# Three edits at once in a convolution-and-gated-unit backward kernel: a new layout of the inverse spectra in DRAM, more of the hidden activations stored, another order of the first loads

## The chip, the cores and the metric

The kernel runs on one core of a Trainium2 chip. The core has TensorE (matrix products into PSUM, called PE in the profile), VectorE (DVE), ScalarE (ACT), GpSimd (POOL), and SyncE (SP), whose queue here issues every data transfer; 16 DMA engines move the data between DRAM and the on-chip memory SBUF. The metric is the time of one execution on the device in microseconds. The time before the change is the median of three runs, 442.43 us (441.31 to 444.41).

## The reference

For 2,048 tokens of width 512 the reference computes the sum of the input, a convolution block and a gated block, both on the normalized input, and then the gradients of that sum with respect to all inputs but one:

```
xn  = layernorm(q)
k_s = causal convolution of k over 4 tokens with shift_k     # per channel
kv  = k_s * v
y   = irfft(rfft(kv, 4096) * rfft(ssm_k, 4096))[:2048]       # long convolution
A   = xn * (y + kv * ssm_D)
h   = (xn @ w_gate) * (xn @ w_up)                            # width F = 1376
out = q + A + h @ w_down
grads = vjp(out)(grad_out)   # q, k, v, shift_k, ssm_k, ssm_D, w_gate, w_up, w_down
```

All data are bfloat16. The long convolution is computed with Fourier transforms written as matrix products, for three signals at once: the filter (with ssm_D added to its first tap), kv, and the incoming gradient dy = xn * grad_out. Three products of the spectra, transformed back, give y, the gradient of kv and the gradient of the filter.

## The kernel before

The 2,048 tokens lie in 16 rows of 128 partitions (R = 16). The work has these stages.

- **First loads and layernorm.** The program queues loads of x, of grad_out transposed (goT), of grad_out (go) and of the weights of the first step (L341 to L355). Warm-up products of a tile of ones run on TensorE meanwhile (L317 to L323). `ln` (L369) makes mean and variance of a row on VectorE, a square root on ScalarE, a reciprocal, and normalizes the row. `tr_rows` (L384) transposes two rows on TensorE.
- **The gated block in steps of F.** F is cut into six steps (NST, of 256 columns and one of 96). Step j runs over the 16 rows two at a time (`mlp_rows`, L391): grad_out times w_down, and xn times w_gate and w_up, then products on VectorE into a ring of SBUF buffers of 24 rows. From the ring come the weight gradients (`dw_gen`, L534). For the last stage the three results per row (h and two gradients) are needed transposed. Steps 0 to 3, and of step 4 the rows below KEEP = 8, are written to a DRAM tensor HD (`hd_store`, L408). The rest stays in the ring: rows 8 to 15 of step 4 and all of step 5, which `turn_gen` (L559) transposes on TensorE, eight blocks of 128x128 at a time, each eight copied back by ScalarE.
- **Stages A and S, the transforms.** `a_gen` (L417) does the first half of the forward transform and writes to the DRAM tensor AX. `s_gen` (L518) reads it in another order, does the second half (`s_B`), multiplies spectra on VectorE (`s_pw`), does the first half of the inverse transform (`s_Bi`) and writes to the DRAM tensor CX, in 16 stores of 768 KB. CX has 128 frequency rows with 32 token rows of 3 KB each, and 64 bytes of padding after each of the 32. Between these products stand those of the gated block's steps and the weight gradients, so that TensorE has other work while one of them waits.
- **Stage F.** Eight groups n of two token rows. `c_load(n)` (L613) reads from CX, for each of 128 frequency rows, the two rows of the group from both halves of the tokens: four runs of 3 KB per partition. `last_dft` does the second half of the inverse transform. `hd_load(m)` (L579) loads row m of HD with a transposing DMA into one of two buffers for even m or the only one for odd m; it moves 640 rows (even m) or 512 (odd m) of 768 elements, and 128 fewer from m = KEEP on. `y_o` and `y_x` (L719, L732) multiply the transposed blocks with the weights wy, which `wy_load` brings in six loads. `c_load(0)` writes over buffers that the last `s_Bi` reads and needs all stores of CX to have landed.

The order in which the instructions stand is not the order of this code. A recording layer (class Eng, L142) collects operations, and `emit` (L180) puts them out in the order of the list PLAN (L32), which also fixes the PSUM banks. All engines, and SyncE's queue of transfers, work through their own share of this list in order. The profile names line 172, the recording layer, for nearly every instruction; they are told apart by tile and shape.

Of the kernel before, what the change touches and what calls it, by code (L numbers as in the profile page):

```python
# [10 lines left out]
BF = mybir.dt.bfloat16  # L11
# [6 lines left out]
S = 2048  # L18
D = 512
F = 1376  # L20
R = 16
NFB = 11
NST = 6
SW = [256, 96, 256, 256, 256, 256]
SF = [0, 1280, 256, 512, 768, 1024]
SB = [0, None, 1, 2, 3, 4]
WO = [12 * sum(SW[:j]) for j in range(NST)]
NCH = 8
RING = 24
KEEP = 8  # L30
EPS = 1e-5
PLAN = "c-lpG0~98^?{<;~UE8*8+qP}nwr$(CZQHi(y?1y2@4NSRzHg?JO!M?fnw*|aCpI7e!~uf1kOtyGd`JKe5(0yOLLxBm5CTF%C<qN<AS{G~@DKqaLL`U`Q6MTrgXoYIVn9rY1*IV|WP|Kb268|W$O-wO9^`_gkOy)@eaH(1pfV(bd{7X|LKP?kRUtW)hr&<}ia<3e3dNv06o=-J0xCcWr~x&h7Sx7H&<RpPNoWDRpboTz&d>mQLtUr{sh}0~fkx088bTZB3*Dd{^n=DQ4oX26Xae0~0i=eu&=vYaQy2>EVIcH?W-tsoz`rm6IzmsF0pnpIM8cUc9MZ!em;fVT5sZL|Fc=oYBp3yoVF;v!$uJty!5CNtOCU4Mf+?^Xrovd51505xEQ94R4d%iYSOL>vD`bIruoAYxeAo+XAOmcNeXtI8z*^V^J7GV3hV}3fzQArc02$#RY=k|q0gl2~I0VPx8)SlGa2QU)5jX+g;WC_pi|`xH!Fjj>Kj0EvfYT5U<6{C$h-aV+cEv<^4IaQ%_z8(|6LiCe&>eeVXzYoP;2*dSk0A-3qojBPlHnit1<CO&5T?MCm<m%PVj4_~PvADB!(P}ML*P^BgLj}WJ_o>I_zXtiC+LU6u|JN)QP>zAHo?)@6dA|j7z~BYP;nDB#}?QUL*hefg@&!M4TizC*bdvHU<V9~v#}#~!Z{cYJx<5YI1|I;0GxpXaTX53!8i|ZLIfOwm9R3-#amDiBVuGMgoUvP-i4yL8dqQxya&bbK19XhSOQC8DU61tu?&{Qa#$XtV+E{&Rk0dY#8ns*W8fOBj&X1$*1(#00&8JyT#K==4mO~57#m-}D_D<p@g>y5xY&^D;|6Siuc0B<p+>k7H{%-^iU+YS)uVm*7T&`+d<XSu5`KUQI36csdYp(EFe6UIop=B<;S}73hwuw!#>F@dvtU*{j7u;Z?!oMs1CL-%%!Ru#H|D{km>2WmLfnh_@fdEwMOXj_(tO;8CvhoW!K-);uj388iMMbB-Nrk(AMfHlypIp?AwI&#_ynKgR(yuf@ddub<M;|+;~RX7@9;f-z}oZ?KjCNmf?x3)e#am96aT^O_%Hs#-}nau3xJ3mF$pOdc?v-xDHMgKFcg-;QFw|#3os%@qVu>6n@~Txh!-$2?Z8Xej0R8?DoLfNDV3%&G>FPlIch=8=`s$c<dlL^QYvamsVNPmr6H7#(o+V?NSP=zWudH;jmpzdsz4Q~5@n|xv>bC%E;@z7C^zMys5FoAQa;L01*jkuqLEaXiqLc_O2w!+Ri-LbmHJaPDnY}kI@O?P6rEyFO^QjeC^p5RMsynEQap-J3Fr(?p@fu(5>paNN@uY#b);l8o?6j4>_n}pElr|{)P~yA1nNoCr~|d58PuI7Q!naFqi81epf0qEu2C&oN3&=(eWl*ChQ`ut8bj-;E3KueG@9nn2AWUZXd~^Xy)=&I(gE5{eP|z@r=_%q4$>CtOBZMbEvId?j5g6B+D<F!B5kFgw3#l^zw{67qy==D&d@K~K}YEdEvB=yhz`>++C>ZLJ3XSSbexXR54uAy=>#pI-*l2<x>zo@yHAfPj*IK!xqB4f-K7NX8zpp!Tw?cxlDMQUnfpT_+*1nUPSFDj>DYyJ&jJfT+;eL0PE&H{+zU$KLb;Sq-E|7>I=Jxe26c3uTxWNay0}}^)eUsv+<UrBgIqWFkv>p&*TeO6y<BhiiTb#{uAdv~`n%8ciiWwtE|q&juPL=l<I=ixF1>q88C*t}$z^s!To(6^vbt<;xXbQxxSXz@tM78T2CkuN<Z`>lu8C{vnz`n#g=^_RTDjKl54Uk`U0GMowR7bixI8YeLzmCxcOzT@H_4fc;wC%q3c5%xs*B(vyD2W3i|AOUy6A4S6H$rb#=0@iWSkr6LWq}XZoC`iP^P;I&Iw6espu-Xcv9I_aaG+6SIt#-A*F_^>1w&!u8y1FX1Tg9tW0$CTxgl;R=7|y-z{+~-E6nag_osnj$7`+Nf?PQtK3|-*hP>+E};~5MO;KF>LN)omq3cU$dX7(xFk~2t#(^oR7orgTvFNQO1WfGLQ1>na@{R-#bu2v<D$q7mt1bTMedfn?bf<G?ykG%V#s~>z(tdXE~ccG0WOw2a%ttUd*WitQx`{`xik`*GfNmwC(m72&LZJBgM{Z}?zlVQ(o1%Uz$qk$oOD?wm7H>?T{b!6a>`kkQqH+da^B^VGLl;^xQtR(^2kMZ$>o*H?usiXS6z9@ClUFYi^LmTMS0;0N&#8tDo7#8FaNkA@~_+IN=ji_?|!*b(ou@ZZ}-O)l}-Y@$sv~(;?1sx)RV}(#nqB19F?Q7<GNB)n1w5eas#O%`(1r$B9&#YYb?eGTr;UE`<&;dQe8rDNNy+xT_Xv_&83cPch#hYymW_LH>oW<+$+~oUc2t{#<h~Su8q8N?_CdRE1l)A`{24td->=-xg+kg`{KIDSJzs;xpvZ1zPk?6TV~4-my72}FUiKaxxWmTpDsENkQf}3vvVwt!*O|_jFxyjLUM3y9wa$=jO=tnBoD{u!IFUcNM26JyWA*A#EE&N^phmK+a={>JXVr(UrE8kWUlOSDS5oilcO#ZkCUM?QRYiJ&cK;@f=rc3vRE>5Dqbq7ISZHIX);C9a4}BLOC&ANkWyTdC(A5ZAk(EZFO*}FmGkjYDZ_<$k<66*T!0JnMp-EZxj3(qqFjzwOA)TbTcrY*<;q;1*GNU)B-MDG)ZnVTR<=nkuEI6BIxmyj{EZv%7Fi*6xj!$L0lY&t$Ur_Wb+{q#l0m#)Hp^f>AwzhNwBnO8l()+;9?m1UH6M^uvQJv@PB|loWVeju(=v+B%4j|!E&08S;k`1J&&vlH$NQxox8Z{_o-fNesn6~Bu(an6d__9)9qGiKxeH&Fu6#jmOE<nG-MI%pke=L&@5@E$&G)1a_vO2CO&&=<KEgNTp&aE2e2kCt6FI@x<s?6rTk=Jo$tnIOr}?Iw;j{cy&hb}i#4qHdyp+cLouA8j{v>bY0$=1y{7NqKXKBXo<h6X4E8LW?adZADF*TOHm5JPzf5>mS&XX8)GMi4}2mD7+RUh(Hp2kk6b11#XA+-sU{v-E!2LF-}I+Jg)*D(5TU|X8Sp*6PN=Gh!hS?6$AjiYlpg3jalyny5C4GypIbRqxXoBW6)X?%^WcX%^L(=Ggy6X;e>s8KYAZsW&%UnA;v-oc4=Cr8y?yqov%6HcUiIlAuSB)Xq7Xfi#(2l)^$;-tEm(`zbS!iRY&XVPVSM^o!^&ZsLmo37+loJO~6R$a}>HHYrdyP93s@Ke60Yk3`~)DN6RGixqQq3b!FZs3i)S3mMyPOC3?6X(-?nnz#pRnDm|d8fYSPh3EEX<mKDx%CZy=KNY%|K<1mjEm|Q{>tUFh?du1Tuh&H1udw>b+^9didsnvX$h^YRkWj4)oQv&OKK-At(~=tcGYfLO1o<h?Ww)AtoGJE+E>eHKkcu-d4TTMfjUSB>jAB<HMFMI(%M=_>*^34s`Yf3F43jBOo!_TU9Ky1rLNMax?0!hT3x5>b%Soy-?~XR>uo)#TXeEc(L*{_r|ES4hiB+aou#vNj?UG2I$sy)LS3XIb(AjF(K<%Q>Np**^>u<y)CSs6C+Sgrpj-8rHqwXsSsUwNZKAKWsXozW+FV=cBW<Zi^qIEO*7`=<=yPqWAN0C@)mPe1Z|Gyas_*ose$w`u&(7*cy{2z9k#*27dQQ)4V!Ng9^`c(T@0!G3DBC4XYA;pnhi+3fZ(+>rr-rbw7Slr6WesWJ?27)Q-}IM;xBQmOPU`?WuK#KQJEIXSmc=o$6B^NCTR|&kajm!&vUpa);@e66qa`hYozjFB$-tsoa*J%vQdnq<Vks?}MYmLz+G1E5%WByzt);UJR^D=0ddp}Ptd!-nik90lS!t_ebu61@w)$4t8dw!8Y)!1HHMKHU!&+K3%VI^WmDRPfR@7SCK+9wGtf95Bwl>JBTO%86Bdn%1wjox_Mp}0}XrrvQHM7yy&YD|$>tLO1qD`{N*3mj!PwQe+tgDT&7B<xu*gP9=)2x>*wdvNw#@aILYs+nx&9GIr$X44zTVq3Qt*x+iHq(aLdYf&F?U2o}4c5=*+78=jhi#K>wo7)zF54D6YFq7!?X;`5&92#XyJ5HOt-Z6G*3I5qF1uxSY`A@}?Y7cB+I+ifdF_+kvvT&?mKYlQFZRv8+IRb5y=|90wEOnccH206VK42KowWY;+RoZ3``7l_X}e%i{5d;gQT-E(=AYUli|!v=41dgG`s4P@`dBRg#>DTpxc<4t_UZftQ~%5M*l&yD&BycUeR%JE2LHz*`HVh-Pw3BECLiCEPwDqs0{_60`OyA^IiJ}l^%pIbKVVsWVxQV4@mYNspWTP>VSP4V#3%RRd{rOP=ke8i4iCP%&*>xjGCr3t>dX2xzML=SYxv^6yszm?_*x!)K406X^(lNEpVzna^?U_i*Vp&0d?R1kxAql%e&5cw@r8VQU%+?pp?p*Sk9G7-d^6w4m-L-|bKl1g_6>X&U&?p&-Th=g#ZUD^{50RqH}pgObl<}d^D}%;Khu}?z5E<s*w69>{cxYi_w%#;Hb34+_H%t-zua&4{rx1r!w>R1{Q$qn@A3=$2*2A`@*DjgzsZmEZT)7y*AMi${b;|!AMyMA7C*+X^ke-2zsisE^ZaVR-=FfQ{Tbib&-VxY8b8XP^)37oztEraYkhBj$e;IB{0)EDU-0Yvb-&eL_V@h*f6+hmH~k~O*kAHX{bPT{Kk>KxRlm$X_3QmL|H9w)8~ihW$3OQI{7Zk=zw#6PTmQ~~@E`qAf6O2E_xx-B-oNpm{0aZrpY&!dYHEQau<(EH0j<n|eZg4&vjt9A!V*9r@K*>7q=EL|KntGA0&sw65CAEN2A-h903757N2vYB`zzUkKtKco{Xcu41sH*t9Do8W)nG^qb^=#WG6$i+2lPJ^2Rv)gzXd6Or3B%>LxQe?mjwNBAo_nd2c-t)AIJbSXbC2x6x95`F+l&xzZMQsh&h;eaFYDj!v7;{kQsCpEY{yD1!D)R7f3LWHUG`)Zz2I#!CC!J1(OZvfC?5TVC4Vb3sz4553vrLHv"  # L32
KB = 1024


@with_exitstack
def kernel(
    ctx: ExitStack,
    tc: tile.TileContext,
    x_d: bass.AP,  # L40
    go_d: bass.AP,
    goT_d: bass.AP,
    k_d: bass.AP,
    v_d: bass.AP,
# [950 lines left out]
```

## Time and profile before

| | |
|---|---|
| median of three runs | 442.43 us (441.31 to 444.41) |
| the profiled execution, its own time | 444.42 us |
| span of the profiled execution | 442.6 us |
| TensorE busy | 423.1 us, 3,179 products |
| VectorE busy | 353.2 us |
| ScalarE busy | 266.0 us |
| DMA moved | 124.12 MB, 280 GB/s on average |
| loads of CX, 8 of 1,536 KB | 8.3 us median from issue to landing |
| stores to CX, 16 of 768 KB | 5.3 us median |
| transposed loads of HD, 16 | 8.7 us median |

Times count from the start of the span. A window's DMA share is the busy time of the 16 DMA engines over the window; as packets can overlap in an engine it can pass 1. Busy time of TensorE is taken from pipelined products whose ends are modelled. The granted clock of TensorE (PEclk) is 1.0 at full speed.

### The profile page before, as it was taken

To read this page: it belongs to the slowest core of one execution; us is meant where nothing else is said; L and a number is where in the kernel's file an instruction comes from. 1 tells how busy PE (TensorE), PEld (TensorE's weight loads), DVE (VectorE), ACT (ScalarE), POOL (GpSimd) and SP (SyncE) were. 2 spreads that over 40 slices of the span, in tenths; PEclk is the share of its full clock that TensorE was granted. 3 is DMA by queue.
4 is the path that set the end of the run, shared out by engine and by line. 5 is a ranking of instruction groups with operands and counts; after the bars stand their busy time and mean duration, and the time that the engine had idled before them with its cause. 6 is when DMAs were issued, how large, how long until landed. Compare 5 with 4: busy or idle time off the path is not lost.

```text
span 442.6 us, 8134 instructions
## 1 busy us (share of the span) xinstructions
PE 423.1 (96%) x3179; PEld 203.9 (46%) x3179; DVE 353.2 (80%) x690; ACT 266.0 (60%) x366; POOL 3.4 (1%) x9
## 2 busy tenths in 40 slices
PE   5999999999999999999999999999999888999895
PEld 3565546745445543334434345465444333444343
DVE  3889577799934899979999994055797959999897
ACT  3796778488652579999999998386324013321311
POOL 1000000000000000000000000100000000000000
PEclk9699999999999999999999999999999999999999
DMA  8988769999856768957578779999999999999992
GB/s 263 408 290 306 287 237 336 342 361 376 314 213 239 279 198 307 315 187 280 211 271 307 285 279 274 282 327 293 294 256 274 277 284 277 275 284 285 239 314 92
DMA packets 96366, 124.12 MB, mean 280 GB/s; under 512 B 53316, under 2 KB 62153, under 8 KB 96328
## 3 DMA queue, kind: packets, MB, share of 16 engines
q1 hardware_dynamic: 96328, 123.60, 87.7%
q8 instruction: 25, 0.41, 0.4%
q14 instruction: 13, 0.11, 0.1%
HBM read 56.57 MB, written 54.04 MB: 250 GB/s over the span
## 4 chain that ended last, share of the span: by engine, by line
PE 71%; DMA 16%; DVE 7%; ACT 2%; SPq 2%; issue 1%; DVEq 0%; ACTq 0%
PE PP L172 71%; DMA big<-HD 8%; DVE big L172 7%; DMA out_dram<-big 2%; DMA AX<-big 2%; ACT big L172 2%; SPq L172 2%; DMA big<-in_x_dram 2%; DMA big<-CX 2%; DVEq L991 0%; ACTq L172 0%; DVEq L172 0%
## 5 line engine op out<-in xcount | busy, mean ns | idle before, releaser
L172 PE MATMUL PP<-big 128*128 128x512 bf16 (+8 forms) x3179 | 423.1, 347 | 14.6 <-DMA big<-HD 5.3
L172 PEld LDWEIGHTS <-big 128*128 128x128 bf16 (+4 forms) x3179 | 203.9, 98 | 233.3 <-issue 69.7
L172 DVE TENSOR_TENSOR big<-big 128x1024 bf16<-128x1024 bf16 (+5 forms) x465 | 267.7, 631 | 52.8 <-ACT big L172 43.3
L172 ACT CAST big<-PP 128x1024 bf16<-128x1024 f32 (+2 forms) x311 | 224.6, 788 | 92.9 <-PE PP L172 81.4
L172 ACT ACTIVATE big<-big 128x512 bf16<-128x512 f32 (+2 forms) x28 | 18.7, 670 | 72.0 <-DVE big L172 54.5
L172 DVE CAST big<-PP 128x512 bf16<-128x512 f32 (+1 forms) x37 | 32.3, 874 | 13.0 <-PE PP L172 11.4
L172 ACT COPY big<-PP 128x1024 bf16<-128x1024 bf16 x25 | 25.1, 1038 | 6.3 <-PE PP L172 6.3
L172 DVE SCALAR_TENSOR_TENSOR big<-big 128x1 f32<-128x1 f32 (+2 forms) x52 | 25.0, 500 | 0.5
L172 DVE TENSOR_TENSOR big<-big,PP 128x512 bf16<-128x512 bf16 (+1 forms) x17 | 10.9, 652 | 7.1 <-PE PP L172 7.0
L172 DVE BATCH_NORM_STATS2 big<-big 128x6 f32<-128x512 bf16 x16 | 10.7, 678 | 6.9 <-DMA big<-in_x_dram 6.9
L172 DVE SCALAR_TENSOR_TENSOR big<-big,PP 128x512 f32<-128x512 bf16 x16 | 10.9, 684 | 4.1 <-PE PP L172 4.1
L172 DVE TENSOR_SCALAR big<-big 128x1 f32<-128x1 f32 (+1 forms) x28 | 7.0, 261 | 0.2
L172 POOL MEMSET big<- 128x1536 bf16 (+2 forms) x3 | 2.8, 950 | 279.1 <-DMA CX<-big 279.1
L172 ACT ACT_TABLE_LOAD x2 | 2.6, 1283 | 0.8 <-PEq L983 0.7
L172 DVE BATCH_NORM_AGGREGATE big<-big 128x2 f32<-128x6 f32 x16 | 2.6, 174 | 0.1
L172 DVE RECIPROCAL big<-big 128x2 f32<-128x2 f32 x8 | 1.3, 157 | 1.3 <-ACT big L172 1.3
L172 DVE DVE_READ_ACCUMULATOR big<-big,PP 128x1 f32 x16 | 1.3, 83 | 0.0
L172 DVE DVE_READ_ACCUMULATOR big<-big 128x1 f32 x16 | 1.3, 83 | 0.0
L172 DVE MEMSET big<- 128x1 f32 (+1 forms) x2 | 0.2, 112 | 0.8 <-PEq L983 0.8
L172 DVE COPY big<-PP 128x1024 bf16<-128x1024 bf16 x1 | 0.7, 692 | 0.0
masks.py:199 POOL TENSOR_SCALAR_AFFINE_SELECT big<-big 128x128 bf16<-128x128 bf16 x1 | 0.3, 294 | 0.0
masks.py:197 POOL MEMSET big<- 128x128 bf16 x1 | 0.2, 205 | 0.3 <-POOLq L983 0.3
(4 smaller groups left out, 0.4 us busy)
## 6 DMA issues: line engine op xcount, KB each, us to landing
AX<-big SPq DMA_DIRECT2D x16, 768.0 KB, 4.8
big<-AX SPq DMA_DIRECT2D x16, 768.0 KB, 5.0
CX<-big SPq DMA_DIRECT2D x16, 768.0 KB, 5.3
big<-CX SPq DMA_DIRECT2D x8, 1536.0 KB, 8.3
out_dram<-big SPq DMA_DIRECT2D x44, 256.0 KB, 3.3
HD<-big SPq DMA_DIRECT2D x14, 768.0 KB, 5.9
big<-in_v_dram SPq DMA_DIRECT2D x16, 256.0 KB, 4.7
big<-in_w_dram SPq DMA_DIRECT2D x4, 768.0 KB, 8.0
```

What stands on the lines that cost most here:

```text
L172: o.fns.append(lambda: f(*[fix(x) for x in a], **{kk: fix(x) for kk, x in k.items()}))
```

## The change

The change has these parts, and a new PLAN that orders everything anew.

- KEEP goes from 8 to 16: all rows of step 4 are written to HD. `turn_gen` has only step 5 left, two more stores of 768 KB to HD are made, and `hd_load` moves 640 or 512 rows for every m.
- CX is laid out by token chunk: 16 blocks, each of which holds 32 x 8 runs of 3 KB and 4 KB of padding. A store of `s_Bi` is split in two, of 384 KB each, one for each of the two frequency groups. `c_load(n)` reads two whole blocks, one run of 12 KB into each of the 128 partitions. The order of frequencies on partitions differs, and the tables of the two transforms are permuted to match.
- The first loads: x rows 0 and 1 come one by one, loads of x and goT alternate in smaller pieces, the load of shift_k (SK) comes last. Rows 0 and 1 have a layernorm each. The square root writes where the reciprocal is made (the tile std is gone). A square root of a constant is computed at the program's start. Sixteen of the 24 short warm-up products are taken out. The small product into c1 is issued in the loop over rows.

In SyncE's queue as it is built, the 640-row load of HD row 0 stood ahead of the last two stores of CX, and the load of row 1 ahead of the first load of CX. After the change the order is: the last stores of CX, row 0 of HD, the first load of CX, the last load of wy, row 1 of HD. Of the six loads of wy, five stand behind the second last group of stores of CX, where two did. The load of HD row 15 had 12 transfers of 256 KB or so behind it, and has 6. In VectorE's order the copy of the first transposed rows stood behind four of the layernorm sums, the last of them of a row of the third load of x; it now stands behind three, the last of them of row 2.

```diff
-KEEP = 8
+KEEP = 16
...
-    CX = dram.tile([128, 32, 3 * D + 32], BF, name="CX")[:, :, 0:3 * D]
+    CX = dram.tile([16, 256 * 3 * D + 2048], BF, name="CX")[:, 0:256 * 3 * D]
...
+    nc.scalar.activation(s1[:, 0:1], eps_t[:], ACTF.Sqrt)
...
-    for i in range(24):
+    for i in range(8):
         now[0] = -40.0 + i
         MM(at0[:, 0:128], lhsT=ones1[:], rhs=ones1[:], start=True, stop=True)
...
-    xload(0, 2); step()
+    xload(0, 1); step()
+    xload(1, 1); step()
+    gtload(1, 1); step()
     ld(Wl[0][:, 1024:3072], w_d[:, 1024:3072]); step()
     xload(2, 2); step()
-    gtload(1, 1); step()
-    xload(4, 4); step()
-    gtload(2, 2); step()
+    gtload(2, 1); step()
+    xload(4, 2); step()
+    gtload(3, 1); step()
+    xload(6, 2); step()
+    gtload(4, 2); step()
+    xload(8, 4); step()
+    gtload(6, 2); step()
+    xload(12, 4); step()
     ld(SK[:].rearrange("p j d -> p (j d)"), bass.AP(tensor=sk_d.tensor, offset=sk_d.offset, ap=[[0, 128], [1, 4 * D]])); step()
-    xload(8, 4); step()
-    gtload(4, 2); step()
-    xload(12, 4); step()
-    gtload(6, 2); step()
...
-        nc.scalar.activation(std[:, gs], mv[:, gs, 1], ACTF.Sqrt, bias=eps_t[:, 0:1], scale=1.0)
-        nc.vector.reciprocal(rstd[:, gs], std[:, gs])
-        if 2 <= r0 <= 8:
-            STT(c1[:, r0 + 1:r0 + 2], mv[:, r0 + 1:r0 + 2, 0], -1.0, rstd[:, r0 + 1:r0 + 2], op0=ALU.mult, op1=ALU.mult)
+        nc.scalar.activation(rstd[:, gs], mv[:, gs, 1], ACTF.Sqrt, bias=eps_t[:, 0:1], scale=1.0)
+        nc.vector.reciprocal(rstd[:, gs], rstd[:, gs])
         for r in range(r0, r0 + n):
             if 2 <= r0 <= 8 and r > r0:
+                STT(c1[:, r:r + 1], mv[:, r:r + 1, 0], -1.0, rstd[:, r:r + 1], op0=ALU.mult, op1=ALU.mult)
...
-            dst = CX.rearrange("(g k) r e -> (k r) g e", k=4)[:, 4 * i + 2 * s:4 * i + 2 * s + 2, :]
-            st(dst, sp["C"][s][:].rearrange("p g t d -> p g (t d)"))
+            for g in range(2):
+                dst = CX.rearrange("a (g b e) -> a g b e", g=32, b=8)[:, 4 * i + 2 * s + g]
+                st(dst, sp["C"][s][:, g].rearrange("p t d -> p (t d)"))
...
-        r0 = 2 * n
-        ld(f["C"].rearrange("q (h r) e -> q h r e", h=2), CX.rearrange("q (h r) e -> q h r e", h=2)[:, :, r0:r0 + 2, :])
+        ld(f["C"].rearrange("p r e -> p (r e)"), CX.rearrange("(j n) (x e) -> x j n e", j=2, x=64)[:, :, n])
...
-                        ln(0, 2)
+                        ln(0, 1)
+                        ln(1, 1)
```

## The prediction

> **What bounds the kernel now.** I read the page first, then the table of busy times by stage, then the list of waits in the last stage, and last the queue's and VectorE's order of time. The page shows TensorE nearly full:
>
> ```profile
> span 442.6 us, 8134 instructions
> ...
> PE 423.1 (96%) x3179; PEld 203.9 (46%) x3179; DVE 353.2 (80%) x690; ACT 266.0 (60%) x366; POOL 3.4 (1%) x9
> ...
> DMA  8988769999856768957578779999999999999992
> ```
>
> Of 442.6 us TensorE is idle in 19.5. The row of the DMA engines says where a second limit comes in: from the 25th slice on it stands at 9 without a break. The table by stage (span, PE, PEld, DVE, ACT, POOL busy, clock, DMA share, GB/s) makes that exact:
>
> ```profile
> 200.00:230.00 30.00, 30.00 (x306) 13.34 (x305) 29.37 (x54) 27.67 (x36) 0.00 (x0) 1.00 0.74 271
> 260.00:290.00 30.00, 29.82 (x235) 14.98 (x237) 10.72 (x21) 18.73 (x26) 1.41 (x2) 1.00 1.00 290
> 290.00:350.00 60.00, 59.48 (x379) 27.95 (x378) 46.36 (x90) 26.58 (x30) 0.00 (x0) 1.00 1.02 286
> 350.00:430.00 80.00, 73.14 (x371) 31.43 (x371) 71.64 (x152) 19.08 (x22) 0.00 (x0) 1.00 1.07 275
> 430.00:443.00 13.00, 7.75 (x52) 4.13 (x50) 9.98 (x25) 2.10 (x3) 0.00 (x0) 0.92 0.34 127
> ```
>
> Three stages have three answers. From about 30 to 290 us TensorE alone sets the pace (30.00 of 30.00 in the first row, DMA at 0.74). From 290 to 430, the last stage F, TensorE and the DMA engines are both at their limit: TensorE loses 0.5 us in the first 60 us and 6.9 in the next 80, 7.4 together. The last row is the end: TensorE runs out of work, and the DMA engines with it. The list of waits in that stage names what it waits for (engine, releaser: us in total, times, longest):
>
> ```profile
> PE PP L172 <- DMA big<-HD: 5.3, 6, 1.5
> PE PP L172 <- DMA big<-CX: 1.3, 2, 1.1
> PE PP L172 <- ACT big L172: 1.0, 2, 0.8
> ```
>
> So the transposed loads of HD, which the change lengthens, are the very thing TensorE waits for. The third place is the start, on VectorE:
>
> ```profile
> 9.13 0.70 DVE L172 BATCH_NORM_STATS2 big<-big 128x6 f32<-128x512 bf16 x1 [1.83 <-DMA big<-in_x_dram]
> ...
> 11.29 0.69 DVE L172 BATCH_NORM_STATS2 big<-big 128x6 f32<-128x512 bf16 x1 [0.54 <-DMA big<-in_x_dram]
> 11.95 0.69 DVE L172 COPY big<-PP 128x1024 bf16<-128x1024 bf16 x1
> ```
>
> The copy of the first transposed rows stands in VectorE's order behind a layernorm sum that waits for x rows 4 to 7; TensorE's first gate/up product starts at 12.70.
>
> **The change part by part.** Sums are made against the profiled execution: 444.42 us, of which 442.6 are the span and 1.8 lie around it. The median of the runs shown is 442.43; I carry the difference over to it.
>
> *All of step 4 stored.* Removed are 48 transposes (8 rows, 3 tensors, 2 blocks) and 6 ScalarE copies of 1,038 ns. A group of 8 transposes shows 0.6 us busy with 219 ns for a single one, so they follow each other at (0.6 - 0.219) / 7 = 54 ns: 48 x 54 = 2.6 us of TensorE, in a stretch where it was busy 29.82 of 30. All of it is on the path: **-2.6**. The copies (6.2 us) go from an engine that is busy 18.73 of 30 there: 0. Added are two stores of 768 KB into HD in the stage with DMA at 0.74: they lie beside TensorE's work, 0. They would cost their 5.9 us each to land only if a load behind them in the queue were late there, and TensorE waits for no load between 100 and 280.
>
> The price stands in F. Rows 8 to 15 are loaded with 640 and 512 rows of HD instead of 512 and 384: 8 x 128 x 768 x 2 bytes = 1.57 MB more through the transposing loads. At the 275 GB/s of the second half of F that is 5.7 us of all DMA engines. By the rows the price of 128 rows is at most 1.15 us: the 640-row load issued at 303.22 lands after 7.9 us, the 384-row one at 420.68 after 5.6, half the difference each, 9.2 us for eight. The lower end is 0, if the loads are early enough. Six of 16 loads made TensorE wait so far, and each row group of F has about 17.5 us of TensorE work (59.48 + 73.14 + 7.75 = 140.4 us, eight groups of two rows) to cover its loads; I take half of the 5.7: **+2.9**.
>
> *Spectra in 12 KB runs.* The eight loads of CX move the same 1.57 MB each, in 128 runs instead of 512. No row shows 12 KB runs. From 100 to 120 us, where mostly 3 KB runs move, the core gets 373 GB/s; from 11.2 to 18.0, with runs of 4 KB and more, 409. So 12.6 MB cost 33.7 against 30.8 us: between 0 and 2.9 us of DMA time saved; I take 1.2, below the middle, since 3 KB runs are near the best row already. With the DMA engines full in F it counts: **-1.2**. The Trainium skill ("DMA: Bandwidth & Descriptors", section "Specifications") puts the least size for full rate at 512 bytes; by that rule 3 KB runs lose nothing and this term would be 0, which makes the sum 1.2 us later. The sixteen stores become 32 of half the size. Each issue holds the queue 0.36 us (1.1 at most), so some 6 us more over a stage in which the queue mostly waits for an engine; nothing late stands behind them, 0. With two instead of one in front of them, the last stores finish issuing perhaps 0.7 us later, and TensorE has filler before it needs CX: 70 products of the weight gradients, some 15 us, stand there in the new order. The first CX load could slip by that much at no cost.
>
> *Queue order into F.* Before, the 640-row load went ahead of the last CX stores and the 512-row one held the queue for 6.74 us ahead of the first CX load; now the first follows the last stores, and the second the first CX load. One long issue stands ahead of the CX load either way: 0. But less of HD is fetched by then, and five of the six loads of the F weights now stand between the second last CX stores and the first CX load or behind it, where two did before. That work falls into the full stage; it is what rival B is made of.
>
> *The start.* Sixteen short warm-up products go; they ran while nothing else could, so 0 by themselves. x rows 0 and 1 come as two loads with a layernorm each, ScalarE's second table load (1.28 us at 7.33) is moved ahead of the data, and in the new order VectorE's copy stands behind the sum of row 2 alone. Rows 2 and 3 now stand behind 1.84 MB instead of 1.57; at the 326 GB/s of the window from 4.35 to 11.18 that is 0.8 us later, 9.9 instead of 9.13. Sum 0.7 and copy 0.7 then end at 11.35: 1.35 us earlier. Against that, by the reciprocal at 13.95 VectorE has done the same list in both orders, and from 18.0 to 24.8 it is busy 6.6 of 6.8. So between 0 and 1.35; I take **-0.7**. TensorE's clock was 0.5 from 11.18 to 18.00, after a wait of 3.3 us for goT. The eight wide warm-ups that precede full clock at 4.35 stay, and a wait of that kind too, so I take the same pattern: 0. The ends: were that stretch at full clock, 6.0 us of busy time would shrink by 3.0; another such stretch would add 3.3. The Trainium skill ("TensorE: Matmul & The Clock Gate", section "What's actually happening") gives 3.4 us of sustained work as the condition for full clock and an idle window of as much for losing it; by that rule the fewer warm-ups, which lengthen the wait, speak against this part, at up to those 3.3 us.
>
> **Sum:** -2.6 + 2.9 - 1.2 - 0.7 = -1.6. 444.42 becomes 442.8; the median 442.43 becomes **440.8**.
>
> **Rivals.** *A, the forecast*: the path stays on TensorE, F loses about 3 us more to HD loads than now.
>
> *B, slower: the DMA engines become the bound of F.* They are already at 1.07. Then all 5.7 us of the longer loads count, and more: the load of the last row stood ahead of 12 transfers of 256 KB before, and now ahead of about 6. The 6 that move in front of it are 1.57 MB, 5.7 us at 275 GB/s; the last row's products, the layernorm's gradient and the last stores (16 us from that load's landing, at 420.68 + 5.6 = 426.3, to the end) all follow it. 442.43 - 4.5 (2.6, 1.2, 0.7) + 11.4 = **449.3**. It passes 1% (446.9) once TensorE's waits in F grow from 7.4 to over 16 us. For it: the share of DMA. Against it: waits of only 7.4 us so far, none over 1.5.
>
> *C, faster: the queue's new order hides the longer loads.* With no new wait, 444.42 - 2.6 - 2.9 - 1.35 = 437.6, or 435.6 of the median; with half of the present HD and CX waits (3.3) gone as well, 432.3. I put the case at **436**. For it: the even rows have two buffers, and in the first 60 us of F, with loads of 640 and 512 rows, TensorE loses only 0.5 us. Against it: DMA work in F grows in sum.
>
> *D, the small parts do nothing*: longer runs move no faster and VectorE's list at the start eats the gain. The forecast without 1.2 and 0.7: 442.7, no change.
>
> **How the numbers follow.** A 0.36, C 0.32, D 0.12, B 0.20. A and D lie within 1% (438.0 to 446.9, about what a measurement of this kernel can tell from no change), with some of A's spread below it and some above. Faster by over 1% is C with a little of A, 0.35; slower is B, 0.20; the rest 0.45. The range takes in most of C and B: 433.5 to 448.5; within A alone it would be 438 to 445.
>
> **What would show it.** Step 4: transposes 48 fewer, TensorE's busy time near 420; HD loads of 640 and 512 rows to the end, waits on them of some 8 us where 5.3 stood. CX: 128 packets a load, to landing under the 8.3 us median. Start: the first gate/up product near 11.4. Wrong would be: a DMA share falling under 1 in F, waits on HD over 14 us or under 3, or a different run of half clock at the start.

## The result: 3.6% slower, and the profile after

The changed kernel takes 458.2 us (median of 4 runs, 456.3 to 462.8) beside 442.8 us for the kernel before in the same runs (441.3 to 444.4). The ratio is 1.036, with a 95% interval of 1.028 to 1.045. The forecast was 440.8 us, with a range up to 448.5: the sign is wrong and the time lies outside the range.

The page of the changed kernel, the lines that answer to those shown of the kernel before (span, busy time by engine, busy tenths of the DMA engines), and with them the granted clock:

```profile
span 456.8 us, 8061 instructions
...
PE 424.3 (93%) x3115; PEld 200.6 (44%) x3115; DVE 351.8 (77%) x691; ACT 259.2 (57%) x361; POOL 3.4 (1%) x9
...
PEclk9999999999999999999999999899989999898998
DMA  8998997979883579879787999999999999999953
```

TensorE has 64 products fewer (48 transposes and 16 warm-ups), and yet its busy time is 1.2 us longer: the row of the clock shows 8s from the 29th slice on, where the kernel before has 9s in all slices but the second (a 6 there, its one stretch of half clock before the end, which is absent here). The idle time grew from 19.5 to 32.5 us. The table by stage (columns as before: span, PE, PEld, DVE, ACT, POOL busy, clock, DMA share, GB/s) says where:

```profile
200.00:230.00 30.00, 30.00 (x317) 12.73 (x316) 29.93 (x56) 28.23 (x36) 0.00 (x0) 1.00 0.89 300
260.00:290.00 30.00, 26.83 (x180) 12.75 (x180) 9.24 (x18) 12.10 (x18) 1.41 (x2) 1.00 1.00 282
290.00:350.00 60.00, 56.88 (x353) 26.63 (x350) 38.46 (x76) 26.12 (x30) 0.00 (x0) 0.94 1.05 272
350.00:430.00 80.00, 71.40 (x354) 29.99 (x353) 65.19 (x137) 18.60 (x21) 0.00 (x0) 0.96 1.08 277
430.00:457.00 27.00, 20.94 (x113) 10.10 (x111) 22.94 (x55) 3.84 (x5) 0.00 (x0) 0.95 0.55 162
```

Up to 260 us little differs in work: TensorE is busy 4.7 us less by 100 us (88.32 against 93.03) and by 260 us (248.21 against 252.91), but 0.9 of that are the warm-ups and some 3.0 the half clock of the kernel before, which stretched its products. The second row is the first loss: 26.83 of 30 us, 29.82 before. Stage F, which opens with the first inverse product of the spectra, begins at 289.4 us (290.0 before), although the new kernel has less to do ahead of it and leaves some 3 us of weight-gradient products for later. From there to the end it takes 167 us; before it was 153. TensorE is busy 9.4 us longer in that stretch (149.9 against 140.4: the products left for later, and the half clock) and idle 5.3 us longer. VectorE has 38.46 us done in the first 60 us of F where it had 46.36, and does the rest at the end (last row). The waits of TensorE in F, from 290 us on:

```profile
PE PP L172 <- DMA big<-HD: 8.6, 6, 2.6
PE PP L172 <- DMA big<-CX: 2.7, 1, 2.7
PE PP L172 <- DVE big L172: 0.3, 1, 0.3
```

They are 11.6 us, 7.6 before, and a wait of 3.2 us for the first load of CX stands just ahead, from 286.2 to 289.4 us:

```profile
289.36 1.72 PE L172 MATMUL PP<-big 128*64 128x512 bf16 x11 [3.17 <-DMA big<-CX]
```

The waits alone do not make 14 us. The runs below take the change apart.

### The profile page after: what moved, and what is told of

The parts are those of the page before. It is cut to its first block, busy times and chain, and to the rows that moved or that the text cites. A ratio compares the mean times of both kernels' runs of the same rounds, so it can differ in the third digit from the quotient of the medians.

```text
span 456.8 us, 8061 instructions
## 1 busy us (share of the span) xinstructions
PE 424.3 (93%) x3115; PEld 200.6 (44%) x3115; DVE 351.8 (77%) x691; ACT 259.2 (57%) x361; POOL 3.4 (1%) x9
## 4 chain that ended last, share of the span: by engine, by line
PE 58%; DMA 22%; DVE 14%; SPq 3%; issue 2%; ACT 1%; DVEq 0%; ACTq 0%
PE PP L172 58%; DVE big L172 14%; DMA big<-HD 6%; DMA big<-in_k_dram 4%; DMA out_dram<-big 3%; SPq L172 3%; DMA AX<-big 2%; DMA big<-in_sk_dram 2%; DMA big<-CX 2%; DMA big<-in_x_dram 1%; DMA big<-KS 1%; ACT big L172 1%; DVEq L996 0%; ACTq L172 0%; DVEq L172 0%
## 5 line engine op out<-in xcount | busy, mean ns | idle before, releaser
L172 PE MATMUL PP<-big 128*128 128x512 bf16 (+9 forms) x3115 | 424.3, 351 | 26.7 <-DMA big<-HD 8.6
L172 PEld LDWEIGHTS <-big 128*128 128x128 bf16 (+5 forms) x3115 | 200.6, 98 | 249.8 <-issue 80.7
L172 ACT ACTIVATE big<-big 128x512 bf16<-128x512 f32 (+3 forms) x30 | 19.1, 642 | 95.0 <-DVE big L172 94.9
L172 DVE CAST big<-PP 128x512 bf16<-128x512 f32 (+1 forms) x37 | 32.2, 873 | 18.2 <-PE PP L172 13.0
L172 ACT COPY big<-PP 128x1024 bf16<-128x1024 bf16 x19 | 18.7, 1023 | 6.0 <-PE PP L172 6.0
L172 DVE RECIPROCAL big<-big 128x2 f32<-128x2 f32 (+1 forms) x9 | 1.4, 153 | 0.4 <-ACT big L172 0.4
```

What stands on the lines that cost most here:

```text
L172: o.fns.append(lambda: f(*[fix(x) for x in a], **{kk: fix(x) for kk, x in k.items()}))
```

## The experiments

### The parts one by one, in the order before

A plan fixes the order of all engines, so each part was put into the kernel before with every other instruction in its old place, and then all of them together. Four runs:

*The layout of the spectra alone.*

```diff
-            dst = CX.rearrange("(g k) r e -> (k r) g e", k=4)[:, 4 * i + 2 * s:4 * i + 2 * s + 2, :]
-            st(dst, sp["C"][s][:].rearrange("p g t d -> p g (t d)"))
+            for g in range(2):
+                dst = CX.rearrange("a (g b e) -> a g b e", g=32, b=8)[:, 4 * i + 2 * s + g]
+                st(dst, sp["C"][s][:, g].rearrange("p t d -> p (t d)"))
```

`c_load` and the tables of the transforms are changed with it, as shown above.

> The kernel before with the new layout of CX alone, in the old order. Theory 1 (the longer loads of HD fill the DMA engines in F and cost most): 440 to 443 us, since a load of CX moves the same bytes. Theory 2 (the new order costs most): 440 to 443 as well. Theory 3 (the layout costs: four stores instead of two hold the queue 4.1 us instead of 1.0 ahead of the first load of CX, and TensorE waits 3.2 us for that load): 446 to 449.

Measured: 449.3 us, ratio 1.011 (1.007 to 1.016).

*All of step 4 stored, alone* (`KEEP = 16`).

> The kernel before with all of step 4 stored (KEEP = 16), in the old order without the 48 transposes. Theory 1 (longer loads of HD): 450 or more, with over 8 us more of TensorE's waits on HD. Theory 2 (order): 440 to 445. Theory 3 (CX layout): 440 to 445.

Measured: 446.3 us, 1.0047 (1.0007 to 1.0088).

*The start edits alone* (first loads, layernorm of rows 0 and 1, warm-ups, early square root).

> The kernel before with the new first loads, the layernorms of rows 0 and 1 apart and the early square root, fewer warm-ups, the rest in the old order. All three theories: within 2 us of the kernel before. If the late load of shift_k costs what the changed kernel's trace shows up to 100 us (4.7 us more of TensorE's idle time, with 0.9 us fewer warm-ups): 445 to 447.

Measured: 443.6 us, 0.998 (0.994 to 1.002).

*All edits, in the order before* (only `PLAN` differs from the changed kernel).

> All edits of the change, but every operation in the old order. Theory 1 (longer loads of HD): over 452, near the changed kernel's 458. Theory 2 (order): 440 to 446, so that over 12 us of the change are the order's. Theory 3 (CX layout): 448 to 452.

Measured: 452.3 us, 1.020 (1.016 to 1.025).

In us of the 443.5 that the kernel before takes in these runs: layout +5.0, step 4 +2.1, start -0.9 (its interval holds 0), which is +6.2; together they cost +9.0. The new order brings the changed kernel from 1.020 to 1.036, another 7 us. So the layout, which was to gain, costs most of the parts, and nearly half of the loss is in no other edit than the order. Each was followed up.

### The layout: its stores cost, its long runs gain nothing

The sync engine's order of time in the run with the layout alone (start us, us, operation), ahead of the first load of CX:

```profile
267.53 7.69 SPq L172 DMA_TRANSPOSE big<-HD  x1
275.32 3.34 SPq L172 DMA_DIRECT2D CX<-big  x4
278.76 5.87 SPq L172 DMA_TRANSPOSE big<-HD  x1
284.86 0.58 SPq L172 DMA_DIRECT2D big<-CX  x1
```

Four stores hold the queue for 3.34 us; before, two held it for 1.03. The load leaves at 284.86 us, 282.57 before, and TensorE, out of other work, stands from 288.8 to 292.0. Two runs take this apart.

*The first load of CX ahead of the second HD load*, nothing else changed. In the sync engine's queue:

```diff
  st(CX ...)  x4
+ c_load(0)
  hd_load(1)
- c_load(0)
```

> The kernel before with the new layout of the inverse spectra alone, as in the run of that part alone (449.3 us), but the load of chunk 0 stands ahead of the second transposing HD load in the sync engine's queue. Theory of the queue (the sixteen added stores hold the queue, so the load of chunk 0 leaves too late, and TensorE runs dry): the load leaves near 281 to 282 us in place of 284.9, TensorE's gap at 289 us falls from 3.2 us to under 1.5 us, the window of half clock behind it is gone, 443 to 446 us. Rival (the layout itself: its stores land later or its load takes longer, wherever the load stands): the gap stays over 2.5 us, 448 to 451 us.

Measured: 446.8 us, 1.005 (1.002 to 1.009). The load left at 282.05 us, TensorE's gap fell to 0.8 us and the half clock behind it was gone. That is about half of the layout's cost, 2.7 us of 5.0 (give or take 2.5, from both intervals), and a little less than the theory asked for.

*The old layout with split stores.* The same count of stores as in the new layout, the same 3 KB runs at the old addresses:

```diff
-            st(dst, sp["C"][s][:].rearrange("p g t d -> p g (t d)"))
+            for g in range(2):
+                st(dst[:, g], sp["C"][s][:, g].rearrange("p t d -> p (t d)"))
```

> The kernel before, with its own layout of the inverse spectra, but each of the 16 stores split into two (32 stores, the same 3 KB runs at the same addresses). Theory of the count (twice as many stores hold the queue twice as long): four stores hold it 2.0 to 3.3 us where two held it 1.0 to 1.3 us, the first CX load leaves 1 to 2 us later, TensorE has a gap of 1 to 3 us near 290 us, 444.5 to 449 us. Rival (the pattern of the new layout's stores makes them slow to issue, not their number): four of these hold the queue no longer than 1.5 us, 442.5 to 444.5 us.

```profile
267.03 6.05 SPq L172 DMA_TRANSPOSE big<-HD  x1
273.19 2.62 SPq L172 DMA_DIRECT2D CX<-big  x4
275.90 4.44 SPq L172 DMA_TRANSPOSE big<-HD  x1
280.57 0.67 SPq L172 DMA_DIRECT2D big<-CX  x1
```

Measured: 442.5 us, 0.997 (0.994 to 1.000). Four stores do hold the queue longer than two (2.62 us), as the theory of the count said, and yet nothing is lost: the load leaves at 280.57. So the number of stores is not the cause. What differs ahead of the first load of CX is the pattern of the stores (16 blocks of 8 runs in place of 128 runs). The issues of these stores on the sync engine (ns, least/median/most), and their row of the page (KB, median us to landing), with the new layout alone, then with the old one and split stores:

```profile
L172 SPq DMA_DIRECT2D CX<-big x32: 523/596/1948, 168.4 to 277.7; - x32
...
CX<-big SPq DMA_DIRECT2D x32, 384.0 KB, 4.5
```

```profile
L172 SPq DMA_DIRECT2D CX<-big x32: 326/426/2225, 168.3 to 274.9; - x32
...
CX<-big SPq DMA_DIRECT2D x32, 384.0 KB, 3.9
```

The new pattern takes 40% longer to issue and 0.6 us longer to land, and both transposing loads beside the last four held the queue longer too (7.69 and 5.87 us against 6.05 and 4.44; 5.63 and 6.74 in the kernel before). The traces' records of the DMA engines show one thing more: from 165 to 282 us, where these stores are most of the 3 KB packets, such a packet took 45.0 ns per KB in the run with split stores and 50.1 with the new layout alone, 56.3 and 62.6 us of the 16 engines. All nine profiles with the old layout lie at 44.4 to 45.8, all eleven with the new one at 49.7 to 51.4. So the new pattern of stores also takes more of the DMA engines' time, ahead of a stage in which their share is full. Whether that is the other 2.3 us of the layout's cost (1.005) no run shows. And the loads themselves got nothing that shows from their 12 KB runs. The page's rows of that transfer (KB, median us to landing), first with the new layout alone, then with the old one and split stores:

```profile
big<-CX SPq DMA_DIRECT2D x8, 1536.0 KB, 8.1
```

```profile
big<-CX SPq DMA_DIRECT2D x8, 1536.0 KB, 7.6
```

In the kernel before it was 8.3, in the run with the first load moved forward 7.5: no order by length of run.

### Step 4: the added bytes cost most of their transfer time

*Step 4 stored, with the old size of load for rows 8 to 15.*

```diff
-        a, b = 128 * (m % 2), 640 if m < KEEP else 512
+        a, b = 128 * (m % 2), 640 if m < 8 else 512
```

> The kernel before with all of F step 4 stored (446.3 us as a part alone), but the eight transposing loads of HD rows 8 to 15 keep the size that they have in the kernel before (512 and 384 rows in place of 640 and 512); the products of these rows then read stale blocks. Everything else, the two added stores and the missing transposes, is as in that part alone. Theory that the added bytes take what the transposes give (1.57 MB at 275 GB/s, 5.7 us, against 2.6 us): 440.5 to 442.5 us. Rival (the bytes are hidden, and the transposes' 2.6 us are lost because something else sets when F ends): 445 to 447.5 us.

This run leaves out 128 rows of each of the eight loads; the products read what the buffer held.

Measured: 441.2 us, 0.994 (0.991 to 0.997). Beside 1.0047 with full loads that is 1.09% or 4.8 us (give or take 2.3, from both intervals) for 1.57 MB, and 0.62% or 2.7 us (1.3 to 4.2) gained by everything else in this part. The waits of TensorE for HD, first with all loads full, then with the short ones:

```profile
PE PP L172 <- DMA big<-HD: 6.2, 5, 2.0
```

```profile
PE PP L172 <- DMA big<-HD: 3.3, 6, 0.8
```

If the loads are late because their buffers come free late, another buffer must help. With all of step 4 stored, ring places of 12 KB are unused in F, room for a second buffer of the odd rows. Two runs:

```diff
-    hdO = place([128, 6, 512], BF, 73 * KB + 7680)
+    hdO = [place([128, 6, 512], BF, a) for a in (73 * KB + 7680, RH + 12288)]
```

*With each odd row's load moved forward, behind the even row's.*

> The kernel before with all of F step 4 stored, a second buffer for the odd HD rows (in the ring places that rows 8 to 15 of step 4 no longer need), and each odd row's transposing load right behind the even row's in the sync queue. In all kernels so far the end comes 22 to 23 us behind the issue of the last transposing HD load. Theory of the chain (load, product, free buffer, next load sets F's pace): the last such load leaves before 415 us (420.9 before), TensorE waits under 2 us for HD, 437 to 442 us. Rival (TensorE's and VectorE's own work set the pace, or the DMA engines do): TensorE's waits turn up elsewhere, 444 to 448 us.

Measured: 453.9 us, 1.023 (1.019 to 1.028). TensorE waited 0.9 us for HD in F, and 8.6 us for CX: the loads of the spectra now stood behind HD loads, in one queue. The wait changed its name and grew.

*With the queue as it was.*

> All of F step 4 stored and the second buffer for the odd HD rows as in the run with two odd buffers, but every instruction stays where it was in the queue (there the loads of the spectra, moved behind the HD loads, came late: TensorE waited 9.7 us for CX). Theory of the chain (a load that no longer waits for the row two before it leaves as soon as the queue reaches it): TensorE's waits for HD fall from 6.2 us to under 3 us, the last HD load leaves before 418 us, 440 to 444 us. Rival (the queue itself, with its stores that wait for VectorE, sets when the HD loads leave): no change against the part alone, 445.5 to 447.5 us.

Measured: 444.6 us, 1.0045 (1.001 to 1.008), as without the buffer. What the sync engine waited for in F, without and with it:

```profile
SPq L172 <- PE PP L172: 56.3, 13, 8.8
```

```profile
SPq L172 <- PE PP L172: 17.4, 7, 4.3
```

The queue waits for TensorE far less, and TensorE waits for HD as long as ever (6.2 and 5.9 us). A load that may leave earlier does not land early enough to show. Together with the short loads, where 4.8 us were saved for 5.7 us of transfer at 275 GB/s (7.0 us of the 16 engines by the packets of the transposing loads, 75.6 against 68.6), this points to the DMA engines as the limit of F in the old order, with a share of 1.02 to 1.09 from 290 to 430 us in the kernel before and in these runs but the one with loads moved forward (0.92 up to 350 us). It is an inference; no run gave F more bandwidth, and a shorter load also holds the queue for less time.

### The new order: its cost lies in F

The changed kernel and the run with all edits in the order before have the same instructions, so an order can be put together from both: the one up to the first inverse product of F, the other from there. The PSUM banks go with the order, as PLAN fixes both: in F some 50 of 402 placements differ between the two.

*New order, then the order before in F.*

> The kernel after the change in its own order up to the first inverse product of F (chunk 0), and from there on all its remaining instructions in the order of the run that had every edit in the order before (452.3 us). Theory that the new order's 6 us lie in F (there VectorE waits 14.4 us for output stores that stand behind transposing HD loads in the sync queue, 1.6 us before): the stretch from the first inverse product to the end falls from 167 us to 158 to 160 us, VectorE's waits for output stores to under 5 us, 449 to 453 us. Rival (they lie in the start: TensorE has 3.6 us less done by 100 us): 456 to 459 us.

*Order before, then the new order in F.*

> The mirror image: every edit, in the order before up to just ahead of the first inverse product of F, and from there on in the new order. Theory that the new order's 6 us lie in F: VectorE waits over 10 us for output stores, 456 to 460 us. Rival (the start): 450 to 453 us.

Measured: 449.9 us, 1.015 (1.009 to 1.021), and 459.5 us, 1.036 (1.032 to 1.041). The order inside F, with its banks, carries all of it, 2.1% between these two. The new order ahead of F costs nothing that shows (1.015 beside 1.020 with the order before throughout). The last transposing load of HD (start us, us), with the order before in F and with the new one:

```profile
423.79 4.35 SPq L172 DMA_TRANSPOSE big<-HD  x1
```

```profile
434.49 4.20 SPq L172 DMA_TRANSPOSE big<-HD  x1
```

The spans end at 445.9 and 456.5 us, 22.1 and 22.0 us behind that issue. In 15 of the 20 profiles the span ends 22.0 to 23.1 us behind it, in two 20.8, in the two with output stores on another engine 25.3 and 25.4, and in the one with odd loads moved forward 26.4. So the last HD load is a good mark of how late F is. That it is what delays the end is not shown by this: the load itself waits for products of TensorE to free its buffer.

### Inside F: five tries, none of which is shown to be the cause

The profile offers several marks of the new order in F. Each was taken away by itself.

*The first wait.* `c_load(0)` ahead of `hd_load(0)` in the changed kernel:

> The kernel after the change, with the load of chunk 0 ahead of the transposing load of HD row 0 in the sync engine's queue (behind the last four CX stores). Theory of the queue: the load leaves near 276 to 277 us in place of 282.2, TensorE's gap of 3.2 us at 286 us and the window of half clock behind it go, HD rows 0 and 1 come some 3 us later and are not missed: 452 to 455 us. Rival (what the order costs lies elsewhere in F, or HD rows 0 and 1 are then missed): the gap only moves to the first products on HD, 456 to 460 us.

Measured: 457.8 us, 1.030 (1.026 to 1.035). The load left at 281.19 us, not at 276 to 277, because it waits until the last stores of CX have landed; the gap at 286 us went. HD row 0 came at 281.85 and TensorE then stood 3.7 us for HD at 331 us.

*The half clock.* Four windows of half clock in F stand each behind a wait of 2.5 us or more. The changed kernel got products that do nothing in those waits:

```diff
             for i in order:
+                for _ in range({1757: 10, 1889: 6, 2086: 6, 2171: 6}.get(i, 0)):
+                    o = fix(ops[i].uses[0][1][0])
+                    real.tensor.matmul(o, lhsT=W2 if o.shape[0] == 64 else W1, rhs=xn[:, 15, :], start=True, stop=True)
                 for fn in ops[i].fns:
```

> The kernel after the change, with idle products put ahead of the four products before which TensorE stood idle for 2.5 us or more (10 ahead of the first, 6 ahead of each of the others, 0.21 us each; they write the bank that the waiting product then overwrites). Theory of the clock (an idle stretch of TensorE of 2.5 us or more is followed by 3.4 us at half clock, which costs 1.7 us each): the four windows of half clock in F are gone, the waits for HD and CX themselves stay, 450 to 453 us. Rival (the windows have another cause, or F is bound by VectorE and the DMA engines so that they cost nothing): 456 to 460 us.

Measured: 459.3 us, 1.033 (1.028 to 1.038). The windows are gone from F up to its last 4 us; the table by stage of this run, to be read beside the third and fourth row of the changed kernel's (clock 0.94 and 0.96):

```profile
290.00:350.00 60.00, 55.73 (x359) 27.34 (x365) 37.12 (x74) 24.89 (x29) 0.00 (x0) 1.00 1.04 288
350.00:430.00 80.00, 70.25 (x358) 30.31 (x363) 64.62 (x134) 20.34 (x23) 0.00 (x0) 1.00 1.09 273
```

From the first HD load to the end it took 181.9 us in place of 183.1. So 6.8 us of lost clock, reckoned as 4 windows of 3.4 us at half speed, were worth about 1 us, and nothing that the intervals separate: in place of the slow products TensorE stood idle or did products that give nothing.

*Output stores off the sync engine's queue*, in the changed kernel and in the one before:

```diff
+    st2 = nc.gpsimd.dma_start
...
-        st(o3[:, rs, :], dv[:])
+        st2(o3[:, rs, :], dv[:])
```

and so for all outputs of F but the weight gradients.

> The kernel after the change, with F's output stores (all but the weight gradients') issued by GpSimd, which does nothing else in F, in place of the sync engine. Theory of the shared queue (in the new order output stores stand behind transposing HD loads that wait for TensorE, VectorE then waits 14.4 us for their buffers, and HD loads stand behind stores that wait for VectorE): VectorE's waits for output stores fall under 5 us, the last transposing load is issued before 428 us (434.1 after), 448 to 453 us. Rival (the new order of TensorE's and VectorE's own work in F costs the 6 us, whatever the queue): 456 to 460 us.

> The kernel before, with F's output stores issued by GpSimd in place of the sync engine. Theory of the shared queue: before, the sync engine waits 14.7 us of F for VectorE's results ahead of stores, with loads behind them; without these the last transposing HD load is issued 2 to 5 us earlier, 438 to 442 us. Rival (the HD loads wait for their buffers anyway, 46 us on TensorE, so the queue costs nothing here): 442.5 to 445 us; GpSimd's stores that take longer to issue would make it more.

Measured: 465.8 us, 1.045 (1.036 to 1.054), and 452.7 us, 1.021 (1.015 to 1.028). Stores from GpSimd made both kernels slower, the one before by 9 us and the changed one by 4 (by the ratios, 1.036 to 1.045, whose intervals overlap) to 7.5 (by the medians), part of it at the end, which came 25.3 and 25.4 us behind the last HD load. By the ratios the two kernels stand 2.4% apart here and 3.6% with the stores in the old queue, by the spans of the profiles 16.7 and 14.2 us. As these go opposite ways and both runs pay a price of their own, they do not settle whether the shared queue has a part in the new order's cost.

*Two products on HD rows back in turn.* In the new order the product of row 0 for the output stands some 12 us behind the product of row 1, and one of row 6 ahead of one of row 5; a row's buffer is free only after its last product.

```diff
  # TensorE's order in F
+ y of row 0 (output)
  y of row 1 (output)
  inverse of chunk 2
- y of row 0 (output)
  ...
+ y of row 5 (input gradient)
  y of row 6 (output)
- y of row 5 (input gradient)
```

> The kernel after the change with two of TensorE's products in F moved: y of the output for row 0 ahead of that of row 1 (with VectorE's sum of it; it stood some 20 us later, behind the products of row 1 and chunk 2's inverse), and the second product of row 5 ahead of the first of row 6. A buffer of HD rows comes free when the last product on its rows is done, so in the new order the transposing loads of rows 4 and 7 leave at 331.2 and 362.6 us, 325.2 and 351.2 us with the order before in F. Theory of the late rows (the new order leaves products of a row behind others, which holds the buffer, and the end follows the last load by 22 to 23 us): row 4's load leaves before 328 us, row 7's before 358 us, the last before 431 us (434.3), 452 to 456 us. Rival (these two are caught up by the next wait): 457 to 460 us.

Measured: 460.3 us, 1.034 (1.027 to 1.040). The loads of rows 4 and 7 left at 333.5 and 367.1 us, later than the 331.0 and 362.3 of the changed kernel, and TensorE got a new wait of 4.4 us for VectorE.

*What VectorE waits for.* The changed kernel's VectorE in F, two lines of its waits:

```profile
DVE big L172 <- DMA out_dram<-big: 14.4, 6, 3.3
DVE big L172 <- ACT big L172: 12.0, 6, 8.0
```

Before, the first of these was 1.6 us. A third buffer for the two tiles whose stores it waits for takes that away:

```diff
+        f["m"].append(place([128, 2, D], BF, RH + 12288)); f["dk"].append(place([128, 2, D], BF, RH + 14336))
...
-        acc = f["dk"][(r0 // 2) % 2]; tmp = f["tmp"]
+        acc = f["dk"][(r0 // 2) % 3]; tmp = f["tmp"]
```

and the same for `m` with `n % 3`.

> The kernel after the change in its own order, with a third buffer each for the two tiles whose output stores VectorE waits for in F (the k gradient's sum dk: 3.3, 2.4 and 2.9 us; the output's sum m: 1.9 and 3.3 us), in ring places that nothing uses in F. Nothing is moved. Theory of the late stores (in the new order these stores stand so late in the sync queue that VectorE stands still for them): VectorE's waits for output stores fall from 14.4 us to under 4 us, VectorE has more done by 350 us, 450 to 455 us. Rival (VectorE catches up or waits for TensorE instead, and the end follows the HD loads): 456.5 to 460 us.

```profile
DVE big L172 <- ACT big L172: 33.6, 9, 18.3
DVE big L172 <- PE PP L172: 10.1, 10, 2.5
DVE big L172 <- DMA big<-in_k_dram: 7.3, 3, 2.8
```

Measured: 455.3 us, 1.029 (1.025 to 1.034). The profiled execution, from which these lines come, was the slowest of its four, 459.3 us. No wait for output stores is left, and VectorE did 38.81 us from 290 to 350 us where it did 38.46. Its waits only have other names: in the changed kernel they add up to 53.9 us from 290 us on (18.2 of which stand under a load of wy), here to 52.8. The interval overlaps that of the changed kernel (1.028 to 1.045), so this is at most a part of the loss, some 3 us by the middle values.

No run gave F the new order of one engine alone, or the new banks alone. Which of TensorE's, VectorE's and the queue's share of the order carries the cost, or the banks, stays open.

### A version from the parts that did not lose

The start edits with the old layout's stores split, step 4 as before:

```diff
-    for i in range(24):
+    for i in range(8):
...
+            for g in range(2):
+                st(dst[:, g], sp["C"][s][:, g].rearrange("p t d -> p (t d)"))
```

> The version that the runs point to: the kernel before with the start edits in the order before (0.998 as a part alone) and with its own layout's 16 stores of the inverse spectra split into 32 (0.997 as a part alone), F step 4 kept as before. If both parts add: 441 to 442.5 us, ratio 0.993 to 0.997. Rival (neither part is more than the measurement's scatter): 0.998 to 1.001.

Measured: 444.3 us, 0.9995 (0.996 to 1.003). Neither part was more than scatter. No version here computes the whole and beats the kernel before clear of scatter.

## Why the prediction was wrong, by its own steps

**What bounds F.** The prediction saw both limits, TensorE and the DMA engines, and put its path on TensorE. The runs point nearer to the DMA engines: added bytes cost most of their transfer time and a free buffer gains nothing that shows; in the new order, full clock for TensorE gains next to nothing either.

**-2.6 us, the transposes.** Right as far as it could be measured: what is left of the step when the loads keep their size is -2.7 us (0.62%, interval -4.2 to -1.3).

**+2.9 us, the longer loads.** The mechanism was right. The size was "I take half of the 5.7"; the runs give 4.8, nearer to the whole, though with 2.3 us either way half is not ruled out.

**-1.2 us, the 12 KB runs.** Wrong in sign: +5.0. The loads landed no sooner than those of the old layout with split stores. On this the Trainium skill ("DMA: Bandwidth & Descriptors", section "Specifications") was right against the step: above 512 bytes it knows no gain, and 3 KB and 12 KB runs showed none (7.6 and 8.1 us). About half of the cost came from the side put at 0: "Each issue holds the queue 0.36 us (1.1 at most) ... nothing late stands behind them, 0", and "The first CX load could slip by that much at no cost". The first load of CX stood behind them, 2.3 us later with the layout alone, and TensorE had run out of filler. The rows it drew on were those of another pattern of store: 0.36 us was the median for stores of 768 KB, two runs from each of 128 partitions; the new stores, half the size, took 0.60, and more of the DMA engines' time too. The rest of the 5.0 has no shown cause.

**-0.7 us, the start.** Not contradicted: as a part alone -0.9, with an interval (-2.6 to +0.7) that holds 0 as well. The first gate/up product came at 11.2 us, near the 11.4 that the prediction had. That the clock's pattern there would stay was not so in the profiled execution, which had no half clock before F: the one wait of 3.3 us became two, of 1.3 and 2.3 us. The last section tells why this differs between executions. (The prediction's times of the clock's steps, 4.35, 11.18 and 18.00, are some 0.2 us late against the trace; no term rests on that.)

**0 us, the new order.** This is the largest failure, some 7 us. The step looked at the order as a matter of the sync engine's queue into F ("One long issue stands ahead of the CX load either way: 0"). The plan reorders TensorE and VectorE through all of F too, and the cost lies in F, 1.036 against 1.015 with the order before from the first inverse product on. Which instructions, or which banks, carry it is open: the first load's place, the half clock, two late products and VectorE's waits for stores each gave nothing that their intervals separate from the changed kernel. That the last HD load is late by as much as the end is shown; what makes it late is not.

**The parts are not additive.** Their sum alone is +6.2, together they cost +9.0. The prediction had no term for that, and 2.8 us is within what the intervals allow.

**Rival B** had the side, the stage and the mark: the last HD load late and the end behind it (13.4 us later, and a span 14.2 us longer). It priced this at 449.3 us with a chance of 0.20, since it counted the longer loads and the six transfers moved ahead of the last one, and nothing of the stores' new pattern or the order of the other engines. Its deciding point was that TensorE's waits in F grow from 7.4 to over 16 us; measured as there, over 290 to 430 us, they are 11.7, and with the wait just ahead of F 14.9. That it had the side is partly luck: the time was lost without the waits that were to show it. VectorE, with more left for the end, and slower matrix products stand beside them.

## What to carry to other kernels

A plan that orders all engines anew is a part of the change in its own right; it can cost more than any edit, and is measured by running the new text in the old order and the old order in one stage. Where the DMA engines' share was at 1 through a stage, here 1.03 to 1.09, 1.57 MB of added bytes cost 4.8 of their 5.7 us of transfer, though only 2.9 us of it show as waits for these loads. And a wait that is named in the list of an engine is not yet time to be gained: with two odd buffers, third buffers and filled gaps the named wait went and another took its place.

## What the runs showed of the hardware that was not expected

**TensorE's clock goes by a grid.** In each profile the changes of the granted clock lie on steps of 3.413 us. Over 20 profiled executions, from 24 to 450 us of each, 2,422 such steps were at full clock; the next step was at half clock after 39 of them, in each of which TensorE had stood idle for 1.96 us or more of the 3.413, and at full clock after 2,383, each with 1.95 us idle or less. So what counted was not the length of a gap but how much of it fell into one step. The run with third buffers shows both. Its table by steps (columns as above; the last but two is the clock):

```profile
327.92:331.33 3.41, 1.89 (x9) 0.69 (x7) 3.41 (x8) 0.49 (x1) 0.00 (x0) 1.00 0.91 209
331.33:334.74 3.41, 2.16 (x10) 1.04 (x12) 2.30 (x8) 0.32 (x1) 0.00 (x0) 1.00 1.05 278
334.74:338.16 3.42, 3.42 (x18) 1.53 (x17) 2.13 (x5) 0.81 (x1) 0.00 (x0) 1.00 1.16 175
...
385.94:389.35 3.41, 1.24 (x7) 0.52 (x7) 2.69 (x5) 2.96 (x4) 0.00 (x0) 1.00 1.06 222
389.35:392.77 3.42, 3.42 (x10) 1.18 (x9) 1.38 (x2) 0.00 (x0) 0.00 (x0) 0.50 1.15 237
392.77:396.18 3.41, 3.41 (x17) 1.54 (x16) 3.12 (x5) 0.00 (x0) 0.00 (x0) 1.00 1.04 212
```

A gap of 2.71 us (329.81 to 332.53) straddles a border, with 1.52 and 1.25 us idle in its steps, and costs no clock. A gap of 2.12 us (386.12 to 388.24) lies in one step and is followed by one at half clock, with 10 products in place of 17. The changed kernel's waits of 2.5 to 3.2 us in F all had their 2 us in one step, and the shorter ones of the kernel before in F, 1.51 us at most, cannot. The grid does not start with the kernel: in the 20 profiles it lies 0.23 to 2.95 us, each time elsewhere, behind multiples of 3.413 us from the span's start. So the same wait can cost this in one execution and not in another. The Trainium skill ("TensorE: Matmul & The Clock Gate", section "What's actually happening") has the window of 3,413 ns that runs by itself, and this agrees; it speaks of an idle window, and here 57% of one was enough.

**Stores issued from GpSimd were dearer.** Moving F's output stores there cost 1.021 (1.015 to 1.028) in the kernel before, although GpSimd had nothing else to do in F and the sync engine 43 issues less. A store took 0.54 us to issue (median) where the sync engine took 0.44, and those of 256 KB 5.6 us to landing where they took 3.3.
